# Two weight blocks converted early, inside the attention, and another order of the rest

## The chip, the cores and the metric

The kernel runs on one core of one Trainium2 chip. The metric is the device time of one execution in microseconds (us). Engines are PE (matrix multiplication), ACT, DVE and POOL (elementwise work) and SP (which issues the DMAs); SBUF is the on-chip memory, PSUM the eight banks that PE writes to.

## The reference

Three stages on 4 x 576 tokens (four sequences, 512 channels), all in float32:

```python
x = windowed_attention(q, k, v)            # 8 heads of 64, each token sees itself and 63 before it
h = relu(x @ w_in);  u, v = h[..., :512], h[..., 512:]
v = (v - mean(v)) / sqrt(var(v) + 1e-6)
v = einsum('ts,bsd->btd', w_spatial, v) + b_spatial[:, None]
x = (u * v) @ w_out
y = x + (relu(x.T @ w_tok1) @ w_tok2).T    # mixes tokens; w_tok1 576x256, w_tok2 256x576
out = y + relu(y @ w_ch1) @ w_ch2          # mixes channels; 512x1536 and 1536x512
```

## The kernel before

Each float32 product is made of three matmuls: both operands are split into a rounded half (ACT casts it) and what is left of it (DVE or POOL subtracts), and the products high x high, high x low and low x high are added in PSUM. Some weights arrive as 64-bit floats. A conversion brings them to float32 in integer steps: ACT scales the upper words (`down`, L72), DVE shifts (L63) and merges the remaining bits (L68, L69).

The activations live transposed in one SBUF tile `U` (128 x 4 x 2304: channel block by token), which holds in turn the gate u, the output of `w_out` and y.

**Attention.** The first 245 us run in an order written by hand: 18 turns n = 0..17, nine for each pair of sequences. A turn transposes the probabilities (`pt`, L285), multiplies them with v (`xo`, L297), computes the scores of turn n+2 (`sc`, L241) and their maxima on DVE (L255), and fills PE with older work from a list: `uv_v`, `uv_u` (products with `w_in`; `uv_u` of the second pair first writes the columns of `U` from 1152 on, and comes from turn 12 on) and `spatial` (L161, two tiles of 14 matmuls; DVE takes a tile out of PSUM with L394, `tmp<-mm,bb`, and multiplies it into `U` with L395). On DVE a turn has, in this order, the normalising of turn n+1 (`snorm`, L272 to L274), then the merging of the attention's output (L312), the maxima, and the spatial tiles as they come. An engine does its own list in order, so an instruction that waits holds up all behind it.

**PSUM.** `psmm` has three banks (spatial, `wout`, `tok2`, `ch1`), the pool beside it five: `psa` in the attention, `psA` after it.

**Token stage, 245 to about 358 us.** From here on a scheduler sets the order on each engine by the order of the program text and by priorities. `wout(c)` (five blocks of 512 tokens: gh/gl splits L641, L642, copy of the result L648), `x2nat` (transposes, nh/nl splits L334, L335), `tok1` (hh/hl, L671, L672) and `tok2` (adds into `U`, L683) run while the weights of the last stage are converted at a lower priority: `load_c1(j)`, six blocks of `w_ch1`, and `load_c2(j)`, six blocks of `w_ch2`. Both begin with the conversion of two 512 KB blocks. For `load_c1`, ACT casts and DVE subtracts 128x1024 (L149) and POOL makes four sums (L716). For `load_c2`, POOL makes four sums (L738), ACT casts four pieces, POOL subtracts (L149) and SP stores the halves to `scr` in DRAM, from where the last stage reads them. A conversion issues the loads of the next one in the list `sources`.

**Channel chunks, 358 to 635 us.** Three chunks of 768 tokens. The first has `load_c1(5)` and `load_c2(5)` in it.

Of the kernel before, what the change touches and what calls it, by code (L numbers as in the profile page):

```python
# [35 lines left out]
def tile_kernel(ctx, tc, qT, kT, kE, v, w_in, wsT, b_sp, w_out, w_t1, w_t2, w_c1, w_c2, outT):  # L36
# [422 lines left out]
    def wv_part(k):  # L459
        return w_part(U[:, k, 1152:2176], w_in[128 * k:128 * k + 128, 512:].unsqueeze(1), wi_h[:, k:k + 1, 512:], wi_l[:, k:k + 1, 512:], 512)  # L460

    E = mybir.EngineType
    with tc.manual_schedule(engines={E.PE, E.SP, E.Activation, E.DVE, E.Pool}):
        wv = [wv_part(k) for k in range(4)]
        wu = [wu_part(ft) for ft in range(4)]

        def go(*ws):
            for w in ws:
                next(w, 0)

# [48 lines left out]
        nc.sync.dma_start(out=bb, in_=bass.AP(b_sp.tensor, b_sp.offset, [[0, P], [1, S]]))
        scores(2)  # L520
        snorm(1)
        smax(2, 0)
        smax(2, 1)
        keep_busy(7, psa.tile([P, 512], F32, tag="xo", name="xo", bufs=1))
        uv_v(*its[0])
        conv, late = {1: (0,), 2: (1, 2), 3: (3,)}, ()
        ws_at = {2: 2, 3: 2, 4: 3, 5: 3}
        for n in range(1, len(its)):
            more, some = n + 2 < len(its), n + 1 < len(its)
            cv = [wu[i] for i in conv.get(n, ())]  # L530
            if n > 1:
                if n + 3 < len(its):
                    load_qk(n + 3)
                if more:
                    load_v(n + 2)
            PT = att_turn(n, busy={1: 2, 2: 8}.get(n, 0))
            go(*late)
            go(*late)
            go(*cv[:1])
            go(*cv[:1])  # L540
            if some:
                sexp(n + 1, 0)
                sexp(n + 1, 1)
                snorm(n + 1)
            go(*cv[:1])
            go(*cv[:1])
            tick()
            left = BUDGET - run_work(1)
            go(*cv[1:])
            att_pv(n, PT)  # L550
            go(*cv[1:])
            if more:
                scores(n + 2)
                smax(n + 2, 0)
                smax(n + 2, 1)
            if n > 1:
                tick()
            late = cv[1:]
            while work and left > 0:
                left -= run_work(1)  # L560
                tick()
            load_ws(ws_at.get(n, 0))
            enable(n)
        while turns:
            tick()
# [25 lines left out]
    def c1_source(j):  # L591
        return [w_c1[:, 128 * r:128 * r + 128].rearrange("(k p) c -> p k c", p=P) for r in (j, j + NJ)]

    def c2_source(j):
        return [w_c2[128 * r:128 * r + 128, :] for r in (j, j + NJ)]

    HW, TW, NJ = 384, 768, 6
    sources = [([w_t1[128 * k:128 * k + 256, :].rearrange("(k p) c -> p k c", p=P)], {}) for k in (0, 2)]
    sources += [([w_t1[512:, :]], dict(rows=64, dup=True))]
    sources += [([w_t2[128 * k:128 * k + 128, c0:c0 + 288]], {}) for k in range(2) for c0 in (0, 288)]  # L600
    sources += [(c1_source(j) if w == 1 else c2_source(j), {}) for w, j in
                ((2, 0), (1, 0), (2, 1), (2, 2), (1, 1), (1, 2), (2, 3), (1, 3), (2, 4), (1, 4), (1, 5), (2, 5))]
    issued = []

    def issue_next():
# [69 lines left out]
    def tok2(b):  # L675
        for d in range(4):
            dc = slice(128 * d, 128 * d + 128)
            for c0 in (0, 288):
                cs = slice(c0, c0 + 288)
                us = U[:, d, b * S + c0:b * S + c0 + 288]  # L680
                ps = psmm.tile([P, 512], F32, tag="mm", name="mm")
                mm3(ps[:, :288], [(ht[b][j][0][:, dc], ht[b][j][1][:, dc], t2_h[:, j, cs], t2_l[:, j, cs]) for j in range(2)])
                nc.vector.tensor_tensor(out=us, in0=ps[:, :288], in1=us, op=ALU.add)  # L683

    scr = tc.dram_tile([8, NJ // 2, P, 2, 2, 256], F32, name="scr")
    sums = tc.dram_tile([NJ, P, 4, 256], F32, name="sums")
    c1 = {}

# [38 lines left out]
    @later  # L727
    def load_c2(j):

        X = [k4() for _ in range(2)]  # L730
        Y = [x.rearrange("p (s c) -> p s c", s=4) for x in X]
        convert(X[0])

        def blk(s, n=1):
            return Y[s // 4][:, s % 4:s % 4 + n, :]

        for o, a, b, op in ((4, 1, 3, ALU.add), (5, 4, 0, ALU.subtract), (6, 0, 1, ALU.subtract), (7, 2, 5, ALU.subtract)):
            nc.gpsimd.tensor_tensor(out=blk(o), in0=blk(a), in1=blk(b), op=op)  # L738
        for s, n in ((0, 1), (2, 2), (4, 2), (6, 2)):
            hl = kp.tile([P, 2, 2, 256], F32R, tag="k4", name="hl", bufs=8)[:, :n]  # L740
            split(hl[:, :, 0, :], hl[:, :, 1, :], blk(s, n), nc.gpsimd)
            nc.sync.dma_start(out=scr[s:s + n, j // 2, :, j % 2].rearrange("s p h c -> p s h c"), in_=f(hl))

    def uin(c, h):
        t0 = TW * c + HW * h
        us = U[:, :, t0:t0 + HW]
        uh = up[h].tile([P, 4, HW], F32R, tag="uh", name="uh")
        ul = up[h].tile([P, 4, HW], F32R, tag="ul", name="ul")
        k0 = 2 if c and h else 0
        split(uh[:, k0:], ul[:, k0:], us[:, k0:])  # L750
        return uh, ul

    def usums(c, u):
# [19 lines left out]

    wout(0)
    run_work(len(work))
    load_c2(0)
    wout(1)
    x2nat(0)
    load_c1(0)
    wout(2)  # L780
    tok1(0)
    load_c2(1)
    x2nat(1)
    wout(3)
    tok2(0)
    load_c2(2)
    load_c1(1)
    wout(4)
    x2nat(2)
    load_c1(2)  # L790
    g_stack.close()

    c1q = pool("c1q", "left", stack=c_stack, bufs=1)
# [2 lines left out]
    hbufs = 4  # L796
    hp = pool("hp2", "right", stack=t_stack, bufs=1)
    tok1(1)
    load_c2(3)
    tok2(1)  # L800
    tok1(2)
    x2nat(3)
    load_c1(3)
    tok1(3)
    with tc.high_priority(offset=-LATER):
        u = [uin(0, 0)]
    load_c2(4)
    tok2(2)
    load_c1(4)
    tok2(3)  # L810
    t_stack.close()
    r_stack.close()

# [98 lines left out]
    for c in range(NTOK // TW):  # L912
# [3 lines left out]
        if c:  # L916
            b11, b12, b21, b22, e = ch1_seven(usums(c, u))
        else:
            b11, b12, b21, b22, e = [], [], [], [], []
            for j in range(NJ):  # L920
                if j == 0:
                    load_c1(5)
                    load_c2(5)
                x, y = ch1(u, j)
                b11.append(x)
                b12.append(y)
                x, y = ch1(u, j + NJ)
# [124 lines left out]
```

## Time and profile before

| | |
|---|---|
| median of three runs | 638.99 us (637.54 to 640.49) |
| the profiled execution | 636.93 us, span of its instructions 635.2 us |
| PE busy | 610.3 us (96% of the span) |
| DVE / ACT / POOL busy | 461.6 / 332.9 / 152.3 us |

The span runs from the first to the last instruction in the trace; 1.7 us of the execution lie around it. A busy PE is not waiting, so the 25 us in which it is not busy are all that a better order can win as long as PE's work stays as it is.

### The profile page before, as it was taken

Reading aid. Unit: us, or ns where it says so; the run is one execution under the profiler, and the core shown is the slowest. Engines: PE = TensorE matmul, PEld = TensorE weight load, DVE = VectorE, ACT = ScalarE, POOL = GpSimd, SP = SyncE. Lnnn points to the kernel's source line nnn. Section 1 sums busy time; section 2 is a strip of 40 time slices with the busy share of each in tenths; the row PEclk is TensorE's granted clock in tenths of the full one; section 3 lists DMA queues with packets and bytes.
Section 4 is the critical chain, followed back from the end, with each engine's and each line's share of the span. In section 5 each row is a group of like instructions: output and inputs, shape, how many; then the busy total and the mean of one; then the engine's idle time right before and its main releaser. Section 6 shows DMA issues by size and latency. Waiting matters only on the chain.

```text
span 635.2 us, 11997 instructions
## 1 busy us (share of the span) xinstructions
PE 610.3 (96%) x4455; PEld 567.5 (89%) x4455; DVE 461.6 (73%) x973; ACT 332.9 (52%) x835; POOL 152.3 (24%) x166
## 2 busy tenths in 40 slices
PE   6798999999999999999899999999999999999997
PEld 3467898998889898888798999999999999999987
DVE  4896857556684688769968972288876998867982
ACT  4776853645664455666464442445543646344550
POOL 6600100100010010666364581041000440002510
PEclk9999999999999999999999999999999999999999
DMA  8843463222330135557662637067434675534772
GB/s 332 293 156 115 138 235 117 76 77 85 107 101 2 37 116 180 174 189 254 238 238 93 233 116 300 0 205 252 149 125 136 224 226 194 182 101 150 265 239 75
DMA packets 46106, 103.60 MB, mean 163 GB/s; under 512 B 4192, under 2 KB 16736, under 8 KB 46048
## 3 DMA queue, kind: packets, MB, share of 16 engines
q1 hardware_dynamic: 46048, 102.84, 47.8%
q8 instruction: 35, 0.57, 0.4%
q14 instruction: 23, 0.19, 0.1%
HBM read 83.95 MB, written 18.87 MB: 162 GB/s over the span
## 4 chain that ended last, share of the span: by engine, by line
PE 65%; DVE 14%; ACT 7%; issue 5%; DMA 4%; POOL 3%; SPq 1%; DVEq 0%; POOLq 0%; ACTq 0%
PE mm L161 29%; PE A L904 17%; PE mm L833 7%; PE A L833 5%; ACT pb L264 3%; PE xo L297 2%; PE pt L285 2%; DMA scr<-hl 2%; DVE k L68 1%; POOL k L738 1%; DVE k L69 1%; PE sc L241 1%; DVE ol L899 1%; DMA U<-in_w_in 1%; DVE k L63 1%
## 5 line engine op out<-in xcount | busy, mean ns | idle before, releaser
L904 PE MATMUL A<-oh,w 128*128 128x384 f32 x480 | 102.7, 334 | 0.0
L886 POOL TENSOR_TENSOR H<-H 128x384 f32<-128x384 f32 x36 | 44.7, 1257 | 182.6 <-DVE ol L899 171.2
L899 DVE TENSOR_TENSOR ol<-H,oh 128x384 fp32r<-128x384 f32 x120 | 79.8, 697 | 10.5 <-ACT oh L898 8.3
L904 PEld LDWEIGHTS A<-oh,w 128*128 128x128 f32 x480 | 85.0, 188 | 0.0
L898 ACT CAST oh<-H 128x384 fp32r<-128x384 f32 x120 | 59.8, 512 | 42.0 <-PE A L904 33.4
L904 PE MATMUL A<-ol,w 128*128 128x384 f32 x240 | 61.3, 336 | 2.2 <-DVE ol L899 2.2
L161 PE MATMUL mm<-ws,nh 128*128 128x288 f32 x320 | 62.1, 297 | 0.3 <-DVE tmp L394 0.3
L161 PEld LDWEIGHTS mm<-ws,nh 128*128 128x128 f32 x320 | 49.9, 188 | 1.0 <-DVE tmp L394 0.6
L363 POOL TENSOR_SCALAR rstd<-mv 128x1 f32<-128x1 f32 x18 | 5.2, 287 | 178.5 <-DVE mv L362 178.3
L904 PEld LDWEIGHTS A<-ol,w 128*128 128x128 f32 x240 | 43.1, 188 | 3.2 <-DVE ol L899 3.1
L886 DVE TENSOR_TENSOR H<-H 128x384 f32<-128x384 f32 x36 | 23.6, 654 | 21.6 <-ACT H L826 19.3
L161 PE MATMUL mm<-ws,nl 128*128 128x288 f32 x128 | 37.7, 295 | 0.0
L264 ACT ACTIVATE pb<-pb,nm 128x128 f32<-128x128 f32 x96 | 37.2, 397 | 0.4 <-DVE nm L255 0.4
L286 ACT COPY PT<-pt 128x512 f32<-128x512 f32 x36 | 19.4, 591 | 31.5 <-PE pt L285 31.5
L272 DVE TENSOR_SCALAR rs<-sm 128x8 f32<-128x8 f32 (+1 forms) x19 | 3.2, 171 | 42.8 <-ACT pb L264 42.7
L161 PE MATMUL mm<-xh,wi_h 128*128 128x384 f32 x96 | 32.8, 341 | 0.7 <-ACT vf L357 0.6
L161 PE MATMUL mm<-xh,wi_l 128*128 128x384 f32 x96 | 32.1, 335 | 0.0
L161 PE MATMUL mm<-xl,wi_h 128*128 128x384 f32 x96 | 32.1, 335 | 0.0
L148 ACT CAST hl<-k 128x512 fp32r<-128x512 f32 (+1 forms) x24 | 13.7, 570 | 32.5 <-DVE k L69 15.8
L161 PE MATMUL mm<-gh,wo_l 128*128 128x512 f32 (+1 forms) x80 | 29.4, 370 | 0.0
L161 PE MATMUL mm<-gl,wo_h 128*128 128x512 f32 (+1 forms) x80 | 29.4, 370 | 0.0
L161 PE MATMUL mm<-gh,wo_h 128*128 128x512 f32 (+1 forms) x80 | 29.3, 376 | 0.0
(183 smaller groups left out, 1703.1 us busy)
## 6 DMA issues: line engine op xcount, KB each, us to landing
w<-scr SPq DMA_DIRECT2D x63, 512.0 KB, 4.3
k<-in_w_c SPq DMA_DIRECT2D x24, 512.0 KB, 5.3
scr<-hl SPq DMA_DIRECT2D x18, 512.0 KB, 5.5
kk<-in_kT SPq DMA_DIRECT2D x16, 384.0 KB, 4.5
k<-sums SPq DMA_DIRECT2D x12, 512.0 KB, 3.3
qq<-in_qT SPq DMA_DIRECT2D x18, 256.0 KB, 3.9
va<-in_v SPq DMA_DIRECT2D x18, 256.0 KB, 3.4
vb<-in_v SPq DMA_DIRECT2D x18, 256.0 KB, 4.0
```

Of the source, the lines that this page charges most:

```text
L63: nc.vector.tensor_scalar(out=xi, in0=xi, scalar1=3, scalar2=None, op0=ALU.logical_shift_left)
L148: nc.scalar.copy(out=hi, in_=x)
L161: nc.tensor.matmul(o, a, c, start=(i == 0), stop=(i == n - 1))
L264: nc.scalar.activation(out=pb[:, h, :], in_=scs[g][:, h - 4 * g, :] if mk is None else pb[:, h, :], func=AF.Exp, scale=SCALE if mk is None ...
L285: nc.tensor.transpose(pt[:, h, :], pb[:, 4 * g + h, :], ident)
L286: nc.scalar.copy(out=PT[:, 4 * g:4 * g + 4, :], in_=pt)
L297: nc.tensor.matmul(xo[64 * e:64 * e + 64, j, 64 * q:64 * q + 64], vt[q][:, hc], PT[:, 4 * e + j, 64 * q:64 * q + 64], start=True, stop=True)
L833: nc.tensor.matmul(o, a, m, start=first and i == 0, stop=i == len(todo) - 1, skip_group_check=True)
L886: eng.tensor_tensor(out=out, in0=a, in1=b, op=ALU.subtract)
L898: nc.scalar.copy(out=oh, in_=blk[j])
L899: nc.vector.tensor_tensor(out=ol, in0=blk[j], in1=f(oh), op=ALU.subtract)
L904: nc.tensor.matmul(acc[d], a, m, start=(first and j == 0 and i == 0), stop=(last and j == NJ - 1 and i == 2), skip_group_check=True)
```

## The change

- `early_c2(j)` for j = 0 and 1 does the work of `load_c2(0)` and `load_c2(1)` during the attention, in place, in the columns 1152 to 2175 of `U` that nothing uses before turn 12. Its steps are hung into the turns by `beside(n, point)`: loads in turn 5 + 3j, `down` in the next, the integer steps on DVE in the turn 7 + 3j ahead of `snorm`, POOL's four sums after that turn's maxima and tiles are listed, ACT's casts and POOL's four subtractions at the turn's end, and six stores from SP at the start of turn 8 + 3j.
- The other ten conversions go in the order c1(0), c1(1), c1(2), c2(2), c2(3), c1(3), c1(4), c2(4), c1(5), c2(5); only c2(5) is left in the first chunk.
- The right half of each `tok2` tile takes its bank from `psA` instead of `psmm`.
- `uin`, which splits the input of a chunk, does so in two pieces of 128x768, and `uin(0, 0)` loses its low priority and comes after `tok2(2)`.

No matmul is added or removed.

```diff
+    def early_c2(j):
...
+        for r, src in zip(raw, c2_source(j)):
+            nc.sync.dma_start(out=r, in_=src.bitcast(I32))
...
+        yield
+        for i, (low, high) in enumerate(parts):
+            down(span(2, 2 * i, 2), high)
+        yield
+        to_f32(span(2, 0, 4), parts)
+        yield
+        for o, a, b, op in C2_SUMS:
+            nc.gpsimd.tensor_tensor(out=val[o], in0=val[a], in1=val[b], op=op)
+        yield
+        homes = ((2, 2, 0, 0, 2), (4, 2, 0, 2, 2), (6, 2, 1, 0, 2), (0, 1, 1, 2, 1))
+        for s, n, r, at, w in homes:
+            nc.scalar.copy(out=span(r, at, n).bitcast(F32R), in_=span(2 + s // 4, s % 4, n))
+        for s, n, r, at, w in homes:
+            x = span(2 + s // 4, s % 4, n)
+            nc.gpsimd.tensor_tensor(out=x.bitcast(F32R), in0=x, in1=span(r, at, n), op=ALU.subtract)
+        yield
...
+        EARLY, FROM = 2, 5
+        side = [early_c2(j) for j in range(EARLY)]
+        at = {(FROM + 3 * j + t, point): side[j] for j in range(EARLY)
+              for t, point in ((0, "mid"), (1, "mid"), (2, "exp"), (2, "mid"), (2, "end"), (3, "start"))}
...
-                ((2, 0), (1, 0), (2, 1), (2, 2), (1, 1), (1, 2), (2, 3), (1, 3), (2, 4), (1, 4), (1, 5), (2, 5))]
+                ((1, 0), (1, 1), (1, 2), (2, 2), (2, 3), (1, 3), (1, 4), (2, 4), (1, 5), (2, 5))]
...
-                ps = psmm.tile([P, 512], F32, tag="mm", name="mm")
+                ps = psA.tile([P, 512], F32, tag="A", name="A") if c0 else psmm.tile([P, 512], F32, tag="mm", name="mm")
...
-        split(uh[:, k0:], ul[:, k0:], us[:, k0:])
+        for k in range(k0, 4, 2):
+            split(uh[:, k:k + 2], ul[:, k:k + 2], us[:, k:k + 2])
```

Where it lands on DVE in turn 7 is one piece of the difference in DVE's order (`ws` are pieces of the spatial weights, `rs` opens the normalising of turn 8):

```order
 L335 TENSOR_TENSOR nl<-vf,nh 128x512
 L103 TENSOR_TENSOR ws<-raw,ws 128x288 x3
+L63 TENSOR_SCALAR U<-U 128x1024
+L68 SCALAR_TENSOR_TENSOR U<-U 128x512
+L69 SCALAR_TENSOR_TENSOR U<-U 128x512
+L68 SCALAR_TENSOR_TENSOR U<-U 128x512
+L69 SCALAR_TENSOR_TENSOR U<-U 128x512
 L272 TENSOR_SCALAR rs<-sm 128x8
 L273 RECIPROCAL rs<-rs 128x8
```

The five integer steps stand between the last old instruction of the turn's first part and the normalising. What comes behind `rs` is as it was before (`val` is a piece of `w_out` under conversion):

```order
L63 TENSOR_SCALAR val<-val 128x256
L274 TENSOR_TENSOR pb<-pb,rs 128x1024
L394 TENSOR_TENSOR tmp<-mm,bb 128x288
L63 TENSOR_SCALAR val<-val 128x256
L68 SCALAR_TENSOR_TENSOR val<-raw,val 128x256
L395 TENSOR_TENSOR U<-tmp,U 128x288
L394 TENSOR_TENSOR tmp<-mm,bb 128x288
L68 SCALAR_TENSOR_TENSOR val<-raw,val 128x256
L69 SCALAR_TENSOR_TENSOR val<-raw,val 128x256
L395 TENSOR_TENSOR U<-tmp,U 128x288
L312 TENSOR_TENSOR xl<-xo,xh 128x4x128
```

Then follow eight instructions for the maxima, whose inputs are scores in PSUM and a mask, and the `L394` of the turn's third spatial tile. Nothing in this piece moved; new is what runs on POOL beside it. On POOL, the changed kernel has in the same turns, between the `rstd` pairs that belong to `uv_v`:

```order
 L363 TENSOR_SCALAR rstd<-mv 128x1
 L364 TENSOR_TENSOR rstd<-rstd,mhalf 128x1
+L496 TENSOR_TENSOR U<-U 128x256 x4
+L503 TENSOR_TENSOR U<-U 128x512 x3
+L503 TENSOR_TENSOR U<-U 128x256
 L363 TENSOR_SCALAR rstd<-mv 128x1
 L364 TENSOR_TENSOR rstd<-rstd,mhalf 128x1
```

Eight instructions of POOL now run in a turn in which it had none but the pairs. In the token stage, ACT had this around the last block of `wout` (`nh` are `x2nat`'s, `ws` the home of c1's halves, `U<-mm` the copies that free `psmm` banks):

```order
L342 CAST nh<-A 64x512
L648 COPY U<-mm 128x512
L148 CAST ws<-k_3917 128x1024
L72 ACTIVATE k_4053<-k_3925 128x512
L648 COPY U<-mm 128x512
L641 CAST gh<-U 128x256
L72 ACTIVATE k_4053<-k_3927 128x512
L641 CAST gh<-U 128x256 x2
L648 COPY U<-mm 128x512
```

and in the changed kernel it has (the copies' line is now L704, the splits' L697):

```order
L148 CAST hl<-k_4061 128x256
L148 CAST hl<-k_4061 128x2x256
L334 CAST nh<-A 128x512
L148 CAST hl<-k_4062 128x2x256
L704 COPY U<-mm 128x512 x2
L148 CAST hl<-k_4062 128x2x256
L72 ACTIVATE k_4145<-k_4070 128x512
L72 ACTIVATE k_4145<-k_4072 128x512
L342 CAST nh<-A 64x512
L704 COPY U<-mm 128x512
L697 CAST gh<-U 128x256 x3
L704 COPY U<-mm 128x512
```

The cast of a c1 block that stood ahead of two copies is gone from this place; the casts of a c2 block, whose inputs POOL makes, stand here now.

## Rows read from the trace of the kernel before

**Rows 1.** The page: busy us, share of the span and instructions of PE.

```profile
PE 610.3 (96%) x4455; PEld 567.5 (89%) x4455; DVE 461.6 (73%) x973; ACT 332.9 (52%) x835; POOL 152.3 (24%) x166
```

**Rows 2.** Stretches: length, busy us (instructions) of PE, PEld, DVE, ACT, POOL, granted clock.

```profile
80.00:130.00 50.00, 49.66 (x472) 46.54 (x471) 28.79 (x109) 26.32 (x96) 2.37 (x6) 1.00 0.40 133
245.00:300.00 55.00, 55.00 (x267) 45.77 (x266) 41.79 (x66) 35.08 (x67) 29.01 (x28) 1.00 0.61 207
300.00:345.00 45.00, 41.01 (x257) 36.77 (x256) 36.69 (x58) 22.53 (x41) 19.18 (x24) 1.00 0.55 197
```

**Rows 3.** Timeline of PE, 302 to 336: start, us, [idle before, releaser].

```profile
302.74 0.40 PE L161 MATMUL mm<-t_h,hh 128*128 128x288 f32 x1 [1.46 <-ACT U L648]
302.98 0.30 PE L161 MATMUL mm<-t_l,hh 128*128 128x288 f32 x1
303.12 0.29 PE L161 MATMUL mm<-t_h,hl 128*128 128x288 f32 x1
...
304.71 0.40 PE L161 MATMUL mm<-t_h,hh 128*128 128x288 f32 x1 [0.24 <-ACT U L648]
...
307.64 0.40 PE L161 MATMUL mm<-t_h,hh 128*128 128x288 f32 x1 [1.43 <-DVE U L683]
...
335.45 0.40 PE L161 MATMUL mm<-t_h,hh 128*128 128x288 f32 x1 [0.87 <-DVE U L683]
```

**Rows 4.** Timeline of ACT and DVE just ahead of those gaps.

```profile
300.61 1.05 ACT L148 CAST ws<-k 128x1024 fp32r<-128x1024 f32 x1 [2.69 <-DVE k L69]
...
305.81 1.28 DVE L68 SCALAR_TENSOR_TENSOR k<-k,k 128x512 int32<-128x512 int32 x2
307.12 0.46 DVE L683 TENSOR_TENSOR U<-mm,U 128x288 f32<-128x288 f32 x1
```

**Rows 5.** Timeline: ACT behind POOL, and DVE idle, earlier in the stage.

```profile
260.82 0.62 ACT L148 CAST hl<-k 128x512 fp32r<-128x512 f32 x1 [2.82 <-POOL k L738]
...
284.33 1.20 DVE L63 TENSOR_SCALAR k<-k 128x1024 int32<-128x1024 int32 x1 [4.52 <-ACT k L72]
```

**Rows 6.** Timeline of DVE, POOL and PE around turn 7.

```profile
85.09 1.20 DVE L103 TENSOR_TENSOR ws<-raw,ws 128x288 fp32r<-128x288 f32 x3 [2.39 <-ACT ws L101]
89.80 0.17 DVE L272 TENSOR_SCALAR rs<-sm 128x8 f32<-128x8 f32 x1 [3.52 <-ACT pb L264]
...
96.43 0.45 DVE L394 TENSOR_TENSOR tmp<-mm,bb 128x288 f32<-128x288 f32 x1
...
96.94 0.54 PE L161 MATMUL mm<-ws,nh 128*128 128x288 f32 x2 [0.34 <-DVE tmp L394]
...
99.54 0.59 ACT L286 COPY PT<-pt 128x512 f32<-128x512 f32 x1 [8.65 <-PE pt L285]
```

**Rows 7.** Timeline: DVE and POOL side by side, and each alone.

```profile
257.21 2.97 DVE L642 TENSOR_TENSOR gl<-U,gh 128x512 fp32r<-128x512 f32 x3
...
257.37 1.12 POOL L738 TENSOR_TENSOR k<-k 128x256 f32<-128x256 f32 x1 [0.63 <-DVE k L69]
258.45 1.18 POOL L149 TENSOR_TENSOR hl<-k,hl 128x256 fp32r<-128x256 f32 x1
...
269.44 1.28 DVE L335 TENSOR_TENSOR nl<-A,nh 128x512 fp32r<-128x512 f32 x2
...
343.53 0.74 POOL L738 TENSOR_TENSOR k<-k 128x256 f32<-128x256 f32 x1 [0.71 <-DVE k L69]
345.62 1.30 POOL L149 TENSOR_TENSOR hl<-k,hl 128x512 fp32r<-128x512 f32 x1
345.64 0.46 DVE L683 TENSOR_TENSOR U<-mm,U 128x288 f32<-128x288 f32 x1 [0.34 <-PE mm L161]
```

**Rows 8.** Timeline of DVE in turn 10.

```profile
130.41 0.17 DVE L272 TENSOR_SCALAR rs<-sm 128x8 f32<-128x8 f32 x1 [6.17 <-ACT pb L264]
...
136.00 0.45 DVE L394 TENSOR_TENSOR tmp<-mm,bb 128x288 f32<-128x288 f32 x1
...
138.18 0.46 DVE L394 TENSOR_TENSOR tmp<-mm,bb 128x288 f32<-128x288 f32 x1 [0.37 <-PE mm L161]
```

More of the change, by code (lines that the diff above doesn't have):

```diff
@@ L460, in wv_part, with c2_source, span @@
         return w_part(U[:, k, 1152:2176], w_in[128 * k:128 * k + 128, 512:].unsqueeze(1), wi_h[:, k:k + 1, 512:], wi_l[:, k:k + 1, 512:], 512)
+    HW, TW, NJ = 384, 768, 6
+    scr = tc.dram_tile([8, NJ // 2, P, 2, 2, 256], F32, name="scr")
+    def c2_source(j):
+        return [w_c2[128 * r:128 * r + 128, :] for r in (j, j + NJ)]
+    C2_SUMS = ((4, 1, 3, ALU.add), (5, 4, 0, ALU.subtract), (6, 0, 1, ALU.subtract), (7, 2, 5, ALU.subtract))
+    def early_c2(j):
+        raw, hi, val = [], [], []
+        for k in range(4):
+            home = U[:, k, 1152:2176]
+            if k < 2:
+                raw.append(home.bitcast(I32))
+                hi += [home.bitcast(F32R)[:, 256 * i:256 * i + 256] for i in range(4)]
+            else:
+                val += [home[:, 256 * i:256 * i + 256] for i in range(4)]
+        def span(r, at, n):
+            return U[:, r, 1152 + 256 * at:1152 + 256 * at + 256 * n]
+        parts = []
+        for r, src in zip(raw, c2_source(j)):
+            nc.sync.dma_start(out=r, in_=src.bitcast(I32))
+            r3 = r.rearrange("p (n w) -> p n w", w=2)
+            parts.append((r3[:, :, 0], r3[:, :, 1]))
+        yield
[14 more added lines that the diff above has]
+        yield
+        for h, blocks in ((0, ((2, 4, 0, 0), (6, 2, 1, 0), (0, 1, 1, 2))), (1, ((4, 4, 3, 0), (2, 2, 2, 2), (0, 1, 2, 0)))):
+            for s, n, r, at in blocks:
+                nc.sync.dma_start(out=scr[s:s + n, j // 2, :, j % 2, h].rearrange("s p c -> p s c"), in_=span(r, at, n).rearrange("p (s c) -> p s c", c=256))
     E = mybir.EngineType
@@ L526, in tile_kernel, with beside @@
         conv, late = {1: (0,), 2: (1, 2), 3: (3,)}, ()
+        EARLY, FROM = 2, 5
+        side = [early_c2(j) for j in range(EARLY)]
+        at = {(FROM + 3 * j + t, point): side[j] for j in range(EARLY)
+              for t, point in ((0, "mid"), (1, "mid"), (2, "exp"), (2, "mid"), (2, "end"), (3, "start"))}
+        def beside(n, point):
+            if (n, point) in at:
+                next(at[n, point], 0)
         ws_at = {2: 2, 3: 2, 4: 3, 5: 3}
@@ L535, in tile_kernel @@
                     load_v(n + 2)
+            beside(n, "start")
             PT = att_turn(n, busy={1: 2, 2: 8}.get(n, 0))
@@ L540, in tile_kernel @@
             go(*cv[:1])
+            beside(n, "exp")
             if some:
@@ L557, in tile_kernel @@
                 tick()
+            beside(n, "mid")
             late = cv[1:]
@@ L562, in tile_kernel @@
             load_ws(ws_at.get(n, 0))
+            beside(n, "end")
             enable(n)
@@ L592, in c1_source @@
         return [w_c1[:, 128 * r:128 * r + 128].rearrange("(k p) c -> p k c", p=P) for r in (j, j + NJ)]
-    def c2_source(j):
-        return [w_c2[128 * r:128 * r + 128, :] for r in (j, j + NJ)]
-    HW, TW, NJ = 384, 768, 6
     sources = [([w_t1[128 * k:128 * k + 256, :].rearrange("(k p) c -> p k c", p=P)], {}) for k in (0, 2)]
@@ L680, in tok2 @@
                 us = U[:, d, b * S + c0:b * S + c0 + 288]
-                ps = psmm.tile([P, 512], F32, tag="mm", name="mm")
+                ps = psA.tile([P, 512], F32, tag="A", name="A") if c0 else psmm.tile([P, 512], F32, tag="mm", name="mm")
                 mm3(ps[:, :288], [(ht[b][j][0][:, dc], ht[b][j][1][:, dc], t2_h[:, j, cs], t2_l[:, j, cs]) for j in range(2)])
                 nc.vector.tensor_tensor(out=us, in0=ps[:, :288], in1=us, op=ALU.add)
-    scr = tc.dram_tile([8, NJ // 2, P, 2, 2, 256], F32, name="scr")
     sums = tc.dram_tile([NJ, P, 4, 256], F32, name="sums")
@@ L735, in blk @@
             return Y[s // 4][:, s % 4:s % 4 + n, :]
-        for o, a, b, op in ((4, 1, 3, ALU.add), (5, 4, 0, ALU.subtract), (6, 0, 1, ALU.subtract), (7, 2, 5, ALU.subtract)):
+        for o, a, b, op in C2_SUMS:
             nc.gpsimd.tensor_tensor(out=blk(o), in0=blk(a), in1=blk(b), op=op)
@@ L775, in tile_kernel @@
     run_work(len(work))
-    load_c2(0)
+    load_c1(0)
     wout(1)
     x2nat(0)
-    load_c1(0)
+    load_c1(1)
     wout(2)
     tok1(0)
-    load_c2(1)
+    load_c1(2)
     x2nat(1)
@@ L786, in tile_kernel @@
     load_c2(2)
-    load_c1(1)
     wout(4)
     x2nat(2)
-    load_c1(2)
+    load_c2(3)
     g_stack.close()
@@ L798, in tile_kernel @@
     tok1(1)
-    load_c2(3)
+    load_c1(3)
     tok2(1)
@@ L802, in tile_kernel @@
     x2nat(3)
-    load_c1(3)
+    load_c1(4)
     tok1(3)
-    with tc.high_priority(offset=-LATER):
-        u = [uin(0, 0)]
     load_c2(4)
     tok2(2)
-    load_c1(4)
+    u = [uin(0, 0)]
     tok2(3)
+    load_c1(5)
     t_stack.close()
@@ L921, in tile_kernel @@
                 if j == 0:
-                    load_c1(5)
                     load_c2(5)
```

## The prediction

> **What bounds the kernel now.** I read the page's busy times first: PE is busy in 96% of the span [rows 1], so a change that leaves PE's work alone can win only what PE waits. The stretches come next, to see where that is: 0.3 us in 80 to 130 us, nothing in 245 to 300, and 45.00 - 41.01 = 4.0 us in 300 to 345 [rows 2]. These 4.0 us lie in the stage in which the weights are converted. PE's timeline shows them as four gaps, 1.46, 0.24, 1.43 and 0.87 us [rows 3]; the reader should look at the releasers. Each time PE waits for a `psmm` bank that ACT (L648) or DVE (L683) has not emptied. A gap costs a little more than its idle time: matmuls of 288 columns follow each other at 0.14 us (302.98 to 303.12), but one that stands alone lasts 0.40 and the next starts only 0.24 later, so about 0.1 is lost behind each gap and some 0.15 ahead of it, 4 x 0.27 = 1.1 in all. The four gaps are worth **5.1 us**.
>
> Why the banks are late is in the timelines of ACT and DVE. ACT sits 2.69 us at 300.61 in the cast of a c1 block whose last merge (L69) DVE has not done, and the copies that free banks are behind that cast [rows 4]. DVE does conversion steps (L68, 1.28 us) before the L683 that PE wants at 307.12 [rows 4]. Earlier, DVE had time: it was idle 4.52 us at 284.33 because ACT's `down` of the next conversion came late, and ACT came late because it sat behind POOL's sums of a c2 block, 2.82 us at 260.82 [rows 5]. So the conversions of `w_ch2`, which go from DVE to POOL and back to ACT, hold up their successors, and the arrears fall due after 300.
>
> **The change part by part.**
>
> *Token stage.* Two c2 conversions leave it and c1(5) comes in. On DVE two sets of the five integer steps go and one set with a subtraction of 1024 columns comes. L63 took 1.20 beside POOL [rows 5], of which some 0.55 are POOL's (below), and a merge 0.64 [rows 4]: 0.65 + 4 x 0.64 = 3.2 us for a set, and 1.2 for the subtraction at the pace of a merge, so DVE has 2 us less to do in a stage of 100. More matters that ACT has no POOL to wait for until c2(2), so that the first three conversions can run in the time in which DVE was idle, and that by 300 us nothing is in arrears. The cast that held two copies up is gone from its place; what stands there now are casts that wait for POOL [the two ACT lists under the change]. Walking through the new order with the old durations I find the copies of the last `wout` block about 1.7 us early and no gap of over half a microsecond. The right halves of `tok2` in `psA` banks help the same gaps (L683 may come later before PE notices), and are not counted again. I take the whole **-5.1 us**; bounds: -5.5 (some small slips beside the four gaps) and 0 (the gaps only move). c1(5) out of the first chunk: nothing, since PE does not wait there.
>
> *Attention, the engines that have time.* ACT's two `down`s and four casts (about 3.6 us a block, by 0.59 for 512 columns) fall into idle time such as the 8.65 us ahead of 99.54 [rows 6]; without it they would delay the copies of the next turn's transposes. The loads stand on SP behind nothing that waits long and are issued a turn ahead of their use; a late one would hold ACT ahead of `uv_u`'s copies. The stores are issued at about 105 us and read after 358; the loads of q, k and v behind them on SP are for two and three turns later. DVE's five steps in turn 7 start when the `ws` pieces are done (85.09 + 1.20 = 86.3) and take 3.2 us, to 89.5; the normalising that is behind them starts at 89.80, when ACT's exponentials are done. They fit into the 3.52 us in which DVE was idle [rows 6]; without that cover they would cost their 3.2. In turn 10 the idle time is 6.17 [rows 8]. Each costs 0.
>
> *Attention, POOL beside DVE.* This is the term that I would not have seen in busy times. Where DVE and POOL both read two operands from SBUF, they take turns: three `gl` of 128x512 need 2.97 us from 257.21, while two `nl`, one of whose operands is in PSUM, need 1.28, that is 0.60 each; and POOL's 128x256 operations take 1.12 and 1.18 there, 0.74 alone [rows 7]. L683, with one operand in PSUM, takes 0.46 in the middle of a POOL subtraction [rows 7]. Three `gl` at 0.60 would be 1.88 (1.28 + 0.60), so the two POOL operations that fell wholly between them cost DVE (2.97 - 1.88) / 2 = 0.55 each. A 128x512 POOL subtraction lasts 1.30 against 0.74, 0.56 more, so I charge 1.1 for it. A block has five of the first and three of the second: 5 x 0.55 + 3 x 1.1 = 6.05 us.
>
> In turn 7 POOL starts when DVE's steps end, at 89.5, and its eight operations need until about 98. From 90.1 DVE has eight instructions with two SBUF operands ahead of the third spatial tile (two L63, L274, two L68, L69, two L395, in the list under the change), and no idle time between them. So each meets a POOL operation. The first sum is over before they begin, and part of a second; I let 6.05 - 0.55 - 0.4 = 5.1 us pass to DVE. L394 of that tile, at 96.43, was already late: PE waited 0.34 for it at 96.94 [rows 6]. So there is nothing to absorb the delay; with a few tenths caught up where maxima run beside POOL, PE loses **+4.8 us** in turn 7. Bounds: 0 (POOL gives way, or DVE's list runs ahead) and +6.1 (every operation in full).
>
> In turn 10 the same POOL work finds another DVE. The steps can start at about 124.3 (130.41 - 6.17), so the sums end before the normalising begins; the subtractions wait for ACT's casts and start at about 132.5. Two L395 before the maxima meet them, at most 1.1 each, and L394 moves from 136.00 to 137 or 138. The tile that needs its bank begins at about 138.2, when PE ends the one that DVE waited for at 138.18 [rows 8]. So **0 us**, bounds 0 and +0.7.
>
> Here the notes have a rule that speaks against the change. The Trainium skill (SBUF — State Buffer, section "Who interferes with whom") says that a DVE instruction with two SBUF inputs contends with a GpSimd instruction that reads SBUF, by an exclusive lock held for the whole instruction. The trace agrees that they exclude each other and that one PSUM operand frees DVE; by the whole instruction a block would hold 5 x 0.74 + 3 x 1.30 = 7.6 us instead of 6.05, and the sum would be some 1.3 us worse.
>
> *Sum.* -5.1 + 4.8 + 0 = -0.3 us against the profiled execution's 636.93, that is 636.6. That execution lies 2.06 below the median of 638.99, so I forecast **638.6 us** for a median. About 0.5%, 3.2 us, is what a measurement of this kernel can tell from no change.
>
> **The rivals.**
>
> *A: both terms as reckoned, chance 0.52.* The gaps after 300 vanish and turn 7 pays nearly as much: 637 to 641 us.
>
> *B: turn 7 is cheap, chance 0.27.* For it: each engine has idle time in the attention (DVE is busy 28.79 of 50 us in 80 to 130 [rows 2]), and if DVE gets ahead of POOL whenever both want to read, POOL's work stretches and DVE's does not. Against it: in [rows 7] both stretch. It gives 638.99 - 5.1 + 0 to 1.3 = 633.9 to 635.2 us.
>
> *C: the token stage gives nothing back, and the kernel is slower, chance 0.13.* The place is ACT between c2(2) and c2(3): four casts whose inputs POOL makes now stand ahead of copies that free `psmm` banks, and each such wait was up to 2.82 us in [rows 5]. Two waits of that size in front of copies would make up for the 5.1 us. With turn 7 unchanged this gives 638.99 + 4.8 = 643.8; it decides for slower as soon as the stage gains less than 1.6 us. Against it: POOL has 2 x 6 us less to do there and DVE delivers earlier.
>
> *D: the change hardly does anything, chance 0.08.* The gaps stay, because DVE's work in the stage falls by only 2 us, and turn 7 costs little: 637.5 to 640.
>
> **How the numbers follow.** The likeliest case is A, and its sum is the forecast. Faster by over 0.5% (below 635.8) is B but for its upper end, and the luckier end of A: 0.27 and 0.03. Slower (above 642.2) is C where the stage gains less than 1.6, 0.08, and the upper end of A, 0.02. The rest, 0.60, is the same within 0.5%. The range reaches from B (633.9 less half a microsecond of scatter) to the middle of C: 633.4 to 642.3. A alone is 637 to 641.
>
> **What would show it.** In the trace of the changed kernel: PE's idle time in 300 to 345 falls from 4.0 us to under 1, without `<-ACT U` or `<-DVE U` gaps of over 0.5. A gap of PE of 3 to 5 us waiting for `DVE tmp` stands near 97 us, with L68 and L395 in that turn twice as long as before, and POOL busy from 89 to 98. No such gap in turn 10. The forecast is wrong if that gap is missing (B), or if gaps behind `hl` casts take the place of the old ones after 290 us (C).

## The result, and the profile after

The changed kernel takes **646.1 us** (645.26 to 646.99, six runs) against 639.15 us (637.54 to 640.49, six runs) of the kernel before; the ratio on record is 1.0116 with a 95% interval of 1.0098 to 1.0133 (the two medians alone give 1.0109). It is slower by 7 us, where 638.6 was forecast, and above the range, which ended at 642.3. The profiled execution takes 646.34 us, with a span of 644.6; that of the kernel before lay 2.2 us under its median, so the two traces differ by 9.4 us and the medians by 7.0. Of all the runs reported below one, of 752.39 us of the kernel "a turn earlier", was in a slow state and is left out of that kernel's median.

The page of the changed kernel shows the busy times, as in [rows 1]:

```profile
PE 612.4 (95%) x4455; PEld 569.8 (88%) x4455; DVE 461.8 (72%) x977; ACT 334.3 (52%) x839; POOL 156.3 (24%) x166
```

They are all but equal. The stretches answer to [rows 2]; after the length come the busy us of PE, PEld, DVE, ACT and POOL, then the granted clock:

```profile
80.00:130.00 50.00, 45.46 (x428) 42.13 (x427) 36.67 (x119) 24.05 (x82) 11.97 (x15) 0.97 0.59 195
...
245.00:300.00 55.00, 52.71 (x270) 44.33 (x269) 44.64 (x76) 31.64 (x59) 22.70 (x20) 1.00 0.53 174
300.00:345.00 45.00, 42.03 (x251) 37.79 (x250) 37.33 (x61) 25.29 (x46) 27.06 (x28) 0.96 0.64 218
```

PE loses 4.5 us in 80 to 130, where it lost 0.3. In the token stage it loses 2.3 before 300 and 3.0 behind it, where it lost 0 and 4.0; what was to be won there was not won. The clock is under 1.00 in two of these stretches. PE's waits, first in 80 to 250 and then in 250 to 360, say for whom (us in total, times, longest):

```profile
PE mm L161 <- DVE tmp L394: 4.5, 1, 4.5
PE pt L285 <- DVE pb L274: 1.5, 2, 0.8
...
PE mm L161 <- DVE hl L728: 2.0, 1, 2.0
PE A L161 <- DVE nl L335: 1.2, 1, 1.2
PE mm L161 <- ACT gh L697: 1.1, 1, 1.1
PE mm L161 <- ACT hh L727: 0.6, 1, 0.6
PE mm L161 <- DVE U L739: 0.4, 2, 0.2
```

The `pb` row was there before. The 4.5 us for `tmp` are turn 7. In the token stage none of the four old waits of [rows 3] is left as it was: PE now waits 5.3 us in all, 4.9 of them for inputs (`nl`, `gh`, `hh`, `hl`) and 0.4 still for `U`.

**Turn 7.** The timelines of PE, DVE and POOL, to be held against [rows 6]:

```profile
102.38 0.53 PE L161 MATMUL mm<-ws,nh 128*128 128x288 f32 x2 [4.46 <-DVE tmp L394]
...
91.62 1.21 DVE L274 TENSOR_TENSOR pb<-pb,rs 128x1024 f32<-128x1024 f32 x1
...
93.51 0.96 DVE L68 SCALAR_TENSOR_TENSOR val<-raw,val 128x256 int32<-128x256 int32 x1
94.39 0.99 DVE L395 TENSOR_TENSOR U<-tmp,U 128x288 f32<-128x288 f32 x1
95.30 0.45 DVE L394 TENSOR_TENSOR tmp<-mm,bb 128x288 f32<-128x288 f32 x1
95.67 1.14 DVE L68 SCALAR_TENSOR_TENSOR val<-raw,val 128x256 int32<-128x256 int32 x1
96.73 1.50 DVE L69 SCALAR_TENSOR_TENSOR val<-raw,val 128x256 int32<-128x256 int32 x1
98.15 1.51 DVE L395 TENSOR_TENSOR U<-tmp,U 128x288 f32<-128x288 f32 x1
...
101.87 0.45 DVE L394 TENSOR_TENSOR tmp<-mm,bb 128x288 f32<-128x288 f32 x1
...
90.80 4.26 POOL L496 TENSOR_TENSOR U<-U 128x256 f32<-128x256 f32 x4 [10.51 <-ACT pb L264]
95.14 5.11 POOL L503 TENSOR_TENSOR U<-U 128x512 fp32r<-128x512 f32 x4
```

In the kernel before, DVE has in the same turn:

```profile
92.04 0.42 DVE L68 SCALAR_TENSOR_TENSOR val<-raw,val 128x256 int32<-128x256 int32 x1
92.37 0.45 DVE L395 TENSOR_TENSOR U<-tmp,U 128x288 f32<-128x288 f32 x1
```

POOL is busy from 90.8 to 100.25. From 93.51 on, each DVE instruction of the list with two SBUF operands takes longer than in the kernel before: about 1 us beside a sum and 1.5 beside a subtraction, some 0.5 and 1.1 more. L394, one of whose operands is in PSUM, keeps its 0.45. Of the eight instructions that the prediction counted, seven are longer, by 4.4 us in all; L274 is not (1.21 against 1.22), although POOL runs beside it, and why is not shown. The L394 of the third tile starts at 101.87, and PE sits still from about 97.9 to 102.38.

What follows the gap was no term of the forecast. The stretches around it, same columns:

```profile
97.60:102.40 4.80, 0.34 (x4) 0.10 (x2) 4.80 (x21) 0.00 (x0) 2.65 (x3) 1.00 0.19 55
102.40:104.00 1.60, 1.60 (x9) 1.60 (x10) 1.57 (x5) 0.00 (x0) 0.00 (x0) 0.73 0.16 28
104.00:106.00 2.00, 2.00 (x11) 1.99 (x10) 1.17 (x3) 0.00 (x0) 0.00 (x0) 0.50 0.29 109
106.00:108.00 2.00, 2.00 (x16) 2.00 (x15) 0.46 (x1) 1.61 (x5) 0.00 (x0) 0.86 0.00 0
```

Just behind the wait the granted clock falls to 0.50, the lower of the two levels (1.2 GHz). At full clock the work of these 5.6 us would have taken 0.73 x 1.6 + 0.50 x 2 + 0.86 x 2 = 3.9, so **1.7 us** are lost to the clock. Turn 7 costs 4.46 - 0.34 + 1.7 = 5.8 us.

**The gap at 332.** The timelines of PE, DVE, ACT and POOL:

```profile
334.41 0.40 PE L161 MATMUL mm<-t_h,hl 128*128 128x288 f32 x1 [1.97 <-DVE hl L728]
...
327.62 0.95 DVE L149 TENSOR_TENSOR ul<-U,uh 128x768 fp32r<-128x768 f32 x1
...
329.32 1.22 DVE L149 TENSOR_TENSOR c1b<-k,c1b 128x1024 fp32r<-128x1024 f32 x1
330.46 1.49 DVE L149 TENSOR_TENSOR ul<-U,uh 128x768 fp32r<-128x768 f32 x1
331.88 1.75 DVE L149 TENSOR_TENSOR c1b<-k,c1b 128x1024 fp32r<-128x1024 f32 x1
333.66 0.69 DVE L728 SCALAR_TENSOR_TENSOR hl<-A,hh 128x512 fp32r<-128x512 f32 x1
...
334.25 0.62 ACT L148 CAST hl<-k 128x512 fp32r<-128x512 f32 x1 [3.89 <-POOL k L793]
...
329.84 2.71 POOL L793 TENSOR_TENSOR k<-k 128x256 f32<-128x256 f32 x2 [3.34 <-DMA sums<-k]
```

`hh` was ready at 330.4, but DVE does a row of subtractions before `hl`: two of c1 blocks, and the second half of `uin` between them. The last two are stretched by c2(4)'s sums on POOL (2.71 us for two that take 0.74 each alone [rows 7]): the half of `uin` takes 1.49 where the one at 327.62 took 0.95, the second c1 block 1.75 where the first took 1.22. That is 1.1 of the 1.97 us; the other 0.9, by this estimate, is the order alone. ACT waits 3.89 us for the same sums, with the next `hh` behind it. Here too the clock falls behind the gap:

```profile
334.00:336.00 2.00, 0.98 (x3) 0.78 (x4) 0.96 (x2) 1.12 (x2) 1.92 (x4) 0.81 0.00 0
336.00:338.00 2.00, 2.00 (x11) 2.00 (x10) 0.09 (x1) 1.02 (x2) 2.00 (x2) 0.50 0.40 155
338.00:340.00 2.00, 2.00 (x14) 2.00 (x14) 1.16 (x1) 0.75 (x2) 1.45 (x2) 0.84 1.04 347
```

That is 0.19 x 2 + 0.50 x 2 + 0.16 x 2 = some 1.7 us again. The stage waits 5.3 - 4.0 = 1.3 us more than before and loses 1.7 to the clock: +3.0. With turn 7 that is 8.8 of the 9.4 us by which the traces differ; the rest lies in the first 60 us, where executions differ by as much. Counted instead by when PE starts the same matmul in the two traces, the changed kernel is 1.0 us behind at 60 us, 7.0 at 130 and 9.4 at 410, so turn 7 costs 6.0 and the token stage 2.4: the terms above are good to about half a microsecond.

### The profile page after: what moved, and what is told of

Same layout as the page of the kernel before. It is cut to its first block, busy times and chain, and to the rows that moved or that the text cites. A ratio compares the mean times of both kernels' runs of the same rounds, so it can differ in the third digit from the quotient of the medians.

```text
span 644.6 us, 12018 instructions
## 1 busy us (share of the span) xinstructions
PE 612.4 (95%) x4455; PEld 569.8 (88%) x4455; DVE 461.8 (72%) x977; ACT 334.3 (52%) x839; POOL 156.3 (24%) x166
## 4 chain that ended last, share of the span: by engine, by line
PE 66%; DVE 14%; ACT 7%; DMA 6%; issue 3%; POOL 2%; SPq 1%; DVEq 0%; ACTq 0%; POOLq 0%
PE mm L161 27%; PE A L958 16%; PE mm L887 8%; PE A L887 6%; ACT pb L264 4%; PE A L161 3%; DMA scr<-hl 2%; PE xo L297 2%; PE pt L285 2%; DVE k L68 1%; DVE k L69 1%; DMA k<-in_w_c 1%; DVE gl L698 1%; DVE pb L274 1%; DMA U<-in_w_in 1%
## 5 line engine op out<-in xcount | busy, mean ns | idle before, releaser
L953 DVE TENSOR_TENSOR ol<-H,oh 128x384 fp32r<-128x384 f32 x120 | 77.2, 676 | 18.2 <-ACT oh L952 16.1
L940 DVE TENSOR_TENSOR H<-H 128x384 f32<-128x384 f32 x36 | 21.0, 583 | 25.1 <-ACT H L880 22.9
L880 ACT ACTIVATE H<-mm 128x384 f32<-128x384 f32 x24 | 11.7, 492 | 34.0 <-PE mm L161 33.8
```

Source lines behind the costliest of these rows:

```text
L880: nc.scalar.activation(out=t, in_=ps, func=AF.Relu)
L940: eng.tensor_tensor(out=out, in0=a, in1=b, op=ALU.subtract)
L953: nc.vector.tensor_tensor(out=ol, in0=blk[j], in1=f(oh), op=ALU.subtract)
```

## The experiments

Ratios are against the kernel before in the same session (638.2 to 638.7 us in each; 639.15 beside the change itself, so between sessions a difference of under 1 us shows nothing). "Token waits" are PE's waits in the stage, as listed by the trace.

| kernel | us | ratio (95%) | wait for `tmp`, 80 to 245 | token waits |
|---|---|---|---|---|
| before | 639.15 | 1 | 0.3 | 4.0 |
| the change | 646.1 | 1.0116 (1.0098 to 1.0133) | 4.5 | 5.3 |
| no POOL work in early blocks | 641.04 | 1.0042 (1.0028 to 1.0056) | 0.3 | 6.0 |
| a turn earlier | 646.11 | 1.0121 (1.0089 to 1.0154) | 2.0 | 5.6 |
| early blocks alone | 648.48 | 1.0163 (1.0139 to 1.0188) | 4.5 | 6.2 |
| tok2 in one pool | 651.28 | 1.0197 (1.018 to 1.0214) | 4.5 | 8.8 |
| before, tok2 in two pools | 639.22 | 1.0013 (1.0004 to 1.0022) | 0.3 | 4.3 |
| c2(4) before c1(3) | 645.25 | 1.0111 (1.0096 to 1.0126) | 4.5 | 5.5 |
| one early block, turn 10 | 636.33 | 0.9974 (0.996 to 0.9988) | 0.6 | 2.3 |
| the change, interleaved | 641.25 | 1.0045 (1.0026 to 1.0063) | 4.5 | 1.8 |
| one early block, c1(5) moved in | 636.55 | 0.9968 (0.9954 to 0.9982) | 0.6 | 2.3 |
| no early block | 638.3 | 1.0004 (0.9988 to 1.0021) | 0.3 | 4.7 |
| no sums | 645.24 | 1.0108 (1.0072 to 1.0145) | 3.2 | 4.5 |
| subtractions a turn later | 639.81 | 1.0017 (1.0002 to 1.0031) | 1.6 | 1.5 |

**No POOL work in the early blocks** (sums and subtractions left out).

```diff
-        for o, a, b, op in C2_SUMS:
-            nc.gpsimd.tensor_tensor(out=val[o], in0=val[a], in1=val[b], op=op)
...
-            nc.gpsimd.tensor_tensor(out=x.bitcast(F32R), in0=x, in1=span(r, at, n), op=ALU.subtract)
```

> The changed kernel without POOL's eight operations per early block (the four sums and the four subtractions are left out, so the two blocks that are stored are not the reference's); DVE's integer steps, ACT's casts, loads and stores stay. Theory lock (POOL and DVE exclude each other while both read two SBUF operands): the gap of 4.5 us at 97.6 and the half clock behind it vanish, some 6.3 us in all, so 639 to 641 us against 646.1; PE's waits in 80 to 130 at most 0.8 us. Rival steps (DVE's own five integer steps make its third tile late): a gap of over 2 us stays and the time is 643 or more. The token stage is the same in both, with its waits of 7 to 8 us.

641.04 us, 5.1 less than the change. DVE's five steps are still there, and the wait is that of the kernel before (80 to 250):

```profile
PE pt L285 <- DVE pb L274: 1.5, 2, 0.8
PE mm L161 <- DVE tmp L394: 0.3, 1, 0.3
...
80.00:130.00 50.00, 49.65 (x469) 46.53 (x468) 36.41 (x126) 28.44 (x97) 2.93 (x7) 1.00 0.60 197
```

The clock is 1.00 throughout 80 to 130. POOL's work beside DVE is what costs in turn 7, and the steps are hidden. The token stage keeps its waits (6.0 us) and a fall of the clock (0.96 in 300 to 345).

**A turn earlier** (`EARLY, FROM = 2, 4`).

> The changed kernel with the early blocks one turn earlier (FROM = 4: integer steps in turns 6 and 9 instead of 7 and 10), in which no spatial tile waits for DVE behind the normalising. Theory lock: POOL's work meets a DVE that nobody waits for, no gap of over 1 us in 80 to 130, 639 to 641.5 us. Rival (any turn pays, since DVE had only 0.7 us idle ahead of its normalising in turn 6 and POOL's rstd for the normalising is queued behind its own eight operations): 643 or more, with waits of PE for pb or for nh/nl tiles.

The waits for `tmp` fall to 2.0 us in two pieces of 0.99 us, so place matters, and the clock stays at 1.00 in 80 to 130. But they do not vanish, and the time is no better: 646.11 us, with single runs from 643.48 to 647.1. Its trace has a wait of 1.9 us at 36 us for `xl` that the others lack, before the first load that the edit moved (64.48 us). On the time this is inconclusive. Neither expectation held in full: no wait is over 1 us, as the theory had it, but the time is the rival's, and the waits are for `tmp` and not for what the rival named.

**The early blocks alone**, with the ten other conversions in the old order (`early_c2` as in the change; c2(0) and c2(1) taken out of the list).

> The kernel before with the early blocks alone (turns 7 and 10); the ten other conversions stay in their old order and places, tok2 in psmm, uin in one piece at its low priority. Turn 7 should cost the same 6.3 us. Theory new order (the token stage's new waits come from the new order of the conversions, uin's place or tok2's banks): the stage, with two conversions less and the old order, waits under 3 us instead of 5 to 6, so 642 to 643.5 us. Rival removal (taking blocks out does not relieve the stage, the gaps only move): waits of 5 us or more there, 645 to 647 us.

648.48 us: the rival's case, and worse. With the same wait in turn 7 (the clock is lower, 0.93 against 0.97 in 80 to 130), taking two blocks out of the old order made its token stage wait 6.2 us instead of 4.0. PE's main waits in 250 to 365, and DVE just ahead of the longest:

```profile
PE mm L161 <- DVE U L739: 3.5, 3, 3.0
PE mm L161 <- DVE hl L728: 1.2, 1, 1.2
...
343.01 1.74 DVE L149 TENSOR_TENSOR ul<-U,uh 128x1536 fp32r<-128x1536 f32 x1
344.67 1.75 DVE L149 TENSOR_TENSOR c1b<-k,c1b 128x1024 fp32r<-128x1024 f32 x1
346.34 0.45 DVE L739 TENSOR_TENSOR U<-mm,U 128x288 f32<-128x288 f32 x1
```

It is the same bunch as at 332 in the changed kernel: subtractions of `uin` and c1 blocks in a row ahead of what PE wants.

**tok2 in one pool.** The change with `psmm` for both halves.

```diff
-                ps = psA.tile([P, 512], F32, tag="A", name="A") if c0 else psmm.tile([P, 512], F32, tag="mm", name="mm")
+                ps = psmm.tile([P, 512], F32, tag="mm", name="mm")
```

> The changed kernel with tok2's right halves back in psmm, as before the change. The scheduler then puts DVE's hl of the second and third token products ahead of the two c1b subtractions and the two ul halves, not behind all four. Theory bunch (the gap at 332 is these four subtractions in front of hl, beside POOL): that gap (2.0 and 0.6 us, and 1.7 us of half clock behind it, 4 us in all) goes, 641.5 to 643.5 us, unless single psmm waits for U come back (up to 2 us). Rival banks (the second pool is what keeps the stage going): waits for U of over 3 us in all and 647 or more. Turn 7 stays as it is in the changed kernel.

651.28 us, 5 more than the change; one wait of 4.4 us for `U` stands where the bunch now precedes L739 and not `hl`. The rival was right: with the other edits in place, the second pool is worth 5 us. The bunch only chooses another victim.

**Before, with tok2 in two pools**, the same edit on the kernel before.

> The kernel before with one edit of the change alone: tok2's right halves take psA banks. The four gaps of the kernel before (5.1 us) were waits for psmm banks. Theory banks: most of them go, 635 to 637 us against 638.2 to 639.2. Rival lists (an engine's list in order is what is late, and the bank is only where it shows): the wait moves to nh/nl, hh/hl or gh, 638 us or more.

639.22 us, no gain. DVE's L683 now costs PE 0.2 us instead of 2.3, but 1.9 us of waits for ACT's copies (L648) stay, and 2.2 us for `uh`, `hl` and `hh` are new: 4.3 us in all. About half has moved, as the rival had it.

**c2(4) before c1(3).**

```diff
-                ((1, 0), (1, 1), (1, 2), (2, 2), (2, 3), (1, 3), (1, 4), (2, 4), (1, 5), (2, 5))]
+                ((1, 0), (1, 1), (1, 2), (2, 2), (2, 3), (2, 4), (1, 3), (1, 4), (1, 5), (2, 5))]
```

> The changed kernel with c2(4) converted ahead of c1(3) and c1(4), whose home c1b comes free only when the last wout block is done (about 325 us), so that two of their subtractions no longer stand ready together in front of hl. Theory bunch: the gap at 332 shrinks from 2.6 us to under 1 and the half clock behind it goes, 642 to 643.5 us. Rival (any order of these lists has some such gap): 645 us or more, with a new gap of over 1.5 us elsewhere. Turn 7 unchanged.

645.25 us, 0.9 less, but with a ratio of 1.0111 against 1.0116 and intervals that overlap: on the time no gain is shown. The wait for `hl` falls from 2.0 to 0.9 us and the clock stays at 1.00 in 300 to 345, but three waits for `nl` make 2.7 us instead of one of 1.2. In this trace the clock is lower around turn 7 than in that of the change (0.93 against 0.97 in 80 to 130), which hides part of the stage's gain. Both theories got a part.

**One early block, in turn 10.**

```diff
-        EARLY, FROM = 2, 5
+        EARLY, FROM = 1, 8
...
+                ((1, 0), (2, 1), (1, 1), (1, 2), (2, 2), (2, 3), (2, 4), (1, 3), (1, 4), (1, 5), (2, 5))]
```

> One early block only, in turn 10 (EARLY = 1, FROM = 8), the turn that cost nothing in the changed kernel; c2(1) is back in the list between c1(0) and c1(1), c2(4) ahead of c1(3), c1(5) back in the first chunk. Theory lock: no gap of over 0.5 us in 80 to 180, so 4.5 to 6.5 us less than the changed kernel before anything in the token stage: 638 to 641 us. Rival (early work costs wherever it is put): waits of over 1 us in 80 to 180.

636.33 us, ratio 0.9974 (0.996 to 0.9988): faster than both kernels (0.3% below the one before), and below the expected 638 to 641, since the stage gained too. The waits for `tmp` are 0.6 us in all against 0.3 before, so the early block adds 0.3, and the token stage waits 2.3 us (245 to 365):

```profile
PE mm L161 <- DVE U L739: 1.0, 1, 1.0
PE mm L161 <- DVE hl L728: 0.7, 1, 0.7
PE mm L161 <- ACT hh L727: 0.6, 1, 0.6
```

**The change, interleaved**: both early blocks in turns 7 and 10, and one c2 between the c1 blocks.

```diff
-                ((1, 0), (1, 1), (1, 2), (2, 2), (2, 3), (1, 3), (1, 4), (2, 4), (1, 5), (2, 5))]
+                ((1, 0), (2, 2), (1, 1), (1, 2), (2, 3), (2, 4), (1, 3), (1, 4), (1, 5), (2, 5))]
```

> The changed kernel (both early blocks, turns 7 and 10) with the list c1(0), c2(2), c1(1), c1(2), c2(3), c2(4), c1(3), c1(4) in the token stage and c1(5), c2(5) in the first chunk: one c2 between the c1 blocks, c1b's blocks last. Theory bunch (three c1 in a row are the gap at 277, two c1b subtractions the one at 332): the stage loses 3 to 5 us by starts instead of 8.8, so 641 to 643 us with turn 7 unchanged. Rival (too few c2 blocks left between the rest, as in the early blocks alone with the old order): 8 us or more lost, 645 or more.

641.25 us, 4.9 less than the change, with the same 4.5 us in turn 7. The stage now waits 1.8 us:

```profile
PE mm L161 <- DVE U L739: 1.0, 1, 1.0
PE A L715 <- DVE nl L335: 0.4, 1, 0.4
PE mm L161 <- DVE gl L698: 0.2, 1, 0.2
PE mm L161 <- DVE hl L728: 0.2, 1, 0.2
```

So with two blocks less the stage can wait 2.2 us less than in the kernel before, about half of what was hoped for; with the order that the change chose it waits longer.

**One early block, c1(5) moved into the token stage** (the last `load_c1` after `tok2(3)`).

> The kernel with one early block (turn 10), with c1(5) moved from the first chunk into the token stage as the change has it, all else kept. Theory arrears (c1(5) brings 5 us of DVE into a stage whose DVE is late): 1 to 3 us more than the kernel with one early block, 637 to 639.5. Rival (it comes last and nobody waits for it): within 0.5 us of it.

636.55 us, within 0.5 us of the kernel without the move: c1(5) is not what hurt the stage.

**No early block** (`EARLY = 0`, c2(0) and c2(1) back in the list after c1(0) and c1(1), the rest as with one early block).

> No early block at all: c1(0), c2(0), c1(1), c2(1), c1(2), c2(2), c2(3), c2(4), c1(3), c1(4), then c1(5), c2(5) in the first chunk, with tok2 in two pools and uin in halves. If what one early block won comes from taking c2(0) out of the stage, this one loses 6 us or more there and takes 638 us or more; if it comes from the order (c1b's blocks last, c1 first), 635.5 to 637.5. The attention is that of the kernel before.

638.3 us, as the kernel before. The stage waits 4.7 us. The order alone is no gain, and with two blocks taken out of the old order there was a loss: as far as these runs go, it takes the order and the block taken out together.

**No sums**: the change with POOL's subtractions only (they work on other columns).

> The changed kernel without POOL's four sums per early block; the four subtractions stay but work on other columns (the stored blocks are not the reference's). By my terms for turn 7 (0.55 for a 256-column operation, 1.1 for a 512-column one) 3 x 1.1 + 0.55 = 3.9 us stay in DVE's way, and the sums' 4 x 0.55 less the half that met nothing go: a gap of 2.8 to 3.6 us instead of 4.5, and 644 to 645.2 us. If a gap that long still drops the clock, the half clock stays; if not, 643.

645.24 us, with 3.2 us in two pieces (1.7 the longest) in place of 4.5, inside the expected 2.8 to 3.6. The clock falls to 0.50 behind them all the same, and the time, as a ratio, is not told from the change's.

**Subtractions a turn later**, on the interleaved order; the second block moves from turns 8 to 11 to turns 9 to 12.

```diff
-        at = {(FROM + 3 * j + t, point): side[j] for j in range(EARLY)
-              for t, point in ((0, "mid"), (1, "mid"), (2, "exp"), (2, "mid"), (2, "end"), (3, "start"))}
+        at = {(FROM + 4 * j + t, point): side[j] for j in range(EARLY)
+              for t, point in ((0, "mid"), (1, "mid"), (2, "exp"), (3 - j, "mid"), (3 - j, "end"), (4 - j, "start"))}
```

> The interleaved order with both early blocks, but the first block's casts, subtractions and stores one turn later (its POOL subtractions then stand behind two rstd pairs, some 114 us) and the second block one turn later altogether (turns 9 to 12). Only the four sums are left in turn 7: by my terms 4 x 0.55 less the part that meets nothing, a gap of 1.5 to 2 us at the third tile instead of 4.5. If a gap that short leaves the clock alone, 4 us less than the interleaved order: 636.5 to 638; if not, 638.5 to 639.5. Rival (the second block in turn 11 is too late for uv_u): a wait of uv_u for the stores at about 160 us and 639 or more.

639.81 us. PE's waits in 80 to 245:

```profile
PE xo L297 <- ACT PT L286: 2.6, 4, 2.0
PE mm L161 <- DVE tmp L394: 1.6, 1, 1.6
...
164.00:166.00 2.00, 2.00 (x20) 1.67 (x15) 1.09 (x3) 2.00 (x8) 1.41 (x2) 0.50 0.90 267
```

The sums alone cost 1.6 us, as expected, and the clock behind that wait is 1.00. But the rival came as well, at its place though not by its wait: ACT does the second block's casts (1.96 us) just ahead of the transposes' copies, PE waits 2.0 us for these at 161, and the clock falls to 0.50 behind it. (ACT also waits 1.8 us for the block's stores, which holds PE up nowhere.) Most of what was won in turn 7 was lost there.

## Why the prediction was wrong, and where it was right

**Turn 7 was right, and its size a little small.** The step "POOL beside DVE" forecast a gap near 97 us, of 4.8 us, with L68 and L395 doubled, POOL busy from 89 to 98 and nothing in turn 10. Measured are 4.46 us, the doubling and the place; turn 10 has no wait of its own. Taking POOL's work away took the gap away, and leaving only the subtractions or only the sums left 3.2 and 1.6 us of it. The prices of 0.55 and 1.1 us fit: L68 took 0.54 us more beside a sum, L395 1.06 beside a subtraction. That L274 would pay too was wrong. What I did not count is the clock behind the gap, 1.7 us: 5.8 instead of 4.8. The rule of the Trainium skill that I weighed (SBUF — State Buffer, "Who interferes with whom") had the mechanism; its whole-instruction price, 1.3 us above mine, so 6.1, would have come nearer, but for another reason.

**The step that failed is the token stage, -5.1 us.** I took the whole of the four old gaps as gain, because what held the copies up had gone from its place and a walk through the new order with old durations found no new gap. Measured is +3.0 us: the stage waits 5.3 us instead of 4.0, for other things, and loses 1.7 to the clock. The walk missed DVE's list: subtractions of c1 blocks and `uin` came in a row ahead of `hl`, and two of them were longer than their old durations by the very thing that I had priced for turn 7, POOL's sums beside them (1.1 of the 1.97 us). Removing work need not help a stage whose engines do their lists in order, as the early blocks alone show: two blocks less in the old order made it worse. The interleaved order shows that part of the gain was there, since the same two blocks less gave 1.8 us of waits and no fall of the clock. Of the differences between the two orders, c2(4) ahead of c1(3) gave nothing by itself that the times can show, and c1(5) nothing where it was tried (with one early block); that leaves c2(2) between the first c1 blocks, or all of it together. The traces speak for c2(2) at one place: in all six kernels with c1(0), c1(1), c1(2) in a row PE waits 0.9 to 1.6 us for `nl` between 273 and 281 us (in the changed kernel behind 4.4 us of conversion steps on DVE), and in none of the others. No run moves c2(2) alone, so that it makes up the rest is argued, not shown.

**The rivals.** Case C had the right sign, and the place it named, ACT's `hl` casts whose inputs POOL makes, has a part: ACT's list made PE wait 1.7 of the 5.3 us, 0.6 for `hh`, behind the wait of 3.89 us for POOL, and 1.1 for `gh` at 298, behind casts that waited 1.58 and 0.35 us for POOL and a `down` that waited 0.91 for stores. DVE's list made the other 3.6. I gave C 0.13, counted it as slower only where the stage gained less than 1.6 us, and did not think that the stage could lose. That bound of 0 on the loss side was the fault of the range, which ended at 642.3, below even the 643.8 that C gives for a stage without gain.

**The second pool** I counted as help that needs no number. On the kernel before it is worth nothing; with the other edits its absence costs 5 us. Terms of this kind do not add.

Left open: why the scheduler puts the c1 subtractions and `uin`'s together, and a place for both early blocks that costs nothing. Two were tried (a turn earlier, subtractions later); each brought its own wait.

## What to carry to other kernels

An engine with idle time is not free help: where POOL and DVE both read two operands from SBUF, most of each POOL operation was added to DVE's list here (some 0.55 us of 0.74, 1.1 of 1.30), so put such work where nobody waits for DVE soon (turn 10 here), not where DVE is merely idle on average. Taking work out of a stage that runs on in-order lists does not shorten it by itself; look at what moves up into its place, and try the order again with the work gone. Bound such a term from both sides, a loss too.

## What the runs showed of the hardware

The clock's answer to a wait was new to me. Behind the waits of 4.46 and of 1.97 and 0.61 us in the changed kernel the granted clock fell to 0.50 and came back some 3 us later, which cost some 1.7 us each time. Behind the 1.6 us wait of the last experiment (97 to 99 us) it stayed at 1.00:

```profile
98.00:100.00 2.00, 0.70 (x5) 0.70 (x6) 2.00 (x14) 0.00 (x0) 0.00 (x0) 1.00 0.14 52
100.00:102.00 2.00, 2.00 (x18) 2.00 (x18) 1.93 (x5) 0.09 (x1) 0.00 (x0) 1.00 0.35 131
```

and the gaps of up to 1.46 us in [rows 3] left it at 1.00 too [rows 2]. It fell behind the 2.0 us wait at 161 in the same experiment, and behind two waits of 1.50 and 1.74 us in the kernel without sums. So the one gap of 4.46 us in turn 7 cost more than its length, and the four gaps of the kernel before, 4.0 us in sum, did not; what decides between them the runs do not show.
